# A decode-attention and gated-MLP kernel: two heads scored at a time, wider rows for v and wq, one softmax per pair of heads

## The chip, the cores and the metric

The kernel runs on one core of a Trainium2 chip. Its engines are TensorE (PE in the profile, with its weight loads as PEld), VectorE (DVE), ScalarE (ACT), GpSimd (POOL) and SyncE (SP), which issues all loads here. The metric is the device time in microseconds of one execution, the median of several runs.

## The reference

One token is decoded. A gate mixes an attention over a long cache with a gated MLP, all in float32:

```python
x: (1, 1, 512)   k_cache, v_cache: (1, 8, 32768, 128)   wq: (512, 4096)   wo: (4096, 512)
w1, w3: (512, 1792)   w2: (1792, 512)

g = sigmoid((x * gate_w).sum(-1))
q = (x @ wq) as 32 query heads of 128          # 4 query heads share one head of the cache
p = softmax(q . k * 128 ** -0.5)               # over 32768 keys
a = (p . v as one row of 4096) @ wo
b = (silu(x @ w1) * (x @ w3)) @ w2
out = g * a + (1 - g) * b                      # (1, 1, 512)
```

The two caches are 134.2 MB each, wq and wo 8.4 MB each, w1, w3 and w2 3.7 MB each: 296 MB to load for a result of 512 numbers.

## The kernel before, in words

**Units.** Each of the 8 cache heads (`HKV`) is cut into four units of 8,192 keys (4 MB). In a unit of k, each of the 128 partitions holds 64 keys of 128 numbers, one contiguous row of 32 KB. The k rows of one load lie 128 KB apart in memory (`kd`, partition p has 256 keys in a row and unit m takes 64 of them); the v rows of one load lie side by side (`vd`).

**Buffers and the load queue.** One pool `stream` has four buffers of 32 KB a partition, and `load` (lines 67 to 70) takes the next one for every k, v, wq half, w1, w3 and w2. All loads are issued by SyncE, in the order of the program. SyncE waits at each until the buffer that it takes has been read by its last reader: for k that is VectorE's transpose (line 187), for v TensorE's matmul (line 288). wo comes per head in rows of 8 KB, through a pool of two buffers (`load_wo`, line 270); for the last head in rows of 2 KB.

**The loop.** It runs 37 times: in step i it issues k unit i and v unit i - 5 (`LAG`), works off k unit i in four quarters, and then v unit i - 5. w1 and w3 come in steps 2 and 3.

**Scores** (`scores`, line 184). For a quarter c of the 128 numbers of each key, VectorE turns the unit in blocks of 32 x 32 (`kt`, line 187, two buffers), and four matmuls, one for each group of 32 columns of the array, multiply it with the head's query window `win` (line 194; x8 in the profile, since a float32 matmul is recorded as two). After the fourth quarter ScalarE copies the bank into `sb` (line 201).

**Softmax.** It is spread over later steps. `defer(n, fn)` puts a function n ticks on, and `tick` runs what is due; there is one tick after each quarter. When a head's four units are scored, `flip` (line 207) brings keys to the partitions, in two banks of eight matmuls each, one tick apart; `top` takes maxima (219); `maxima`, `diagonal` and `spread_max` bring the maximum over all partitions to all of them (229, 234, 236, 241), one tick each; `softmax` (245) has ScalarE write eight exponentials of 128 x 128 into `prob`, each with its sum by accumulator; `norm` and `invert` make the reciprocal of the sums. The order of the instructions of an engine is that of the program (a manual schedule), so what stands ahead in it and waits holds up all that is behind it on that engine.

**Values** (`values`, line 280). 16 matmuls per v unit add to one bank `o`; after the fourth unit ScalarE copies it to a row (294). `heads` (300) sums over groups, `scaled` (306) multiplies with the reciprocal, `quarter` (318) and `quartered` (325) spread the head over the partitions as wo's rows need it, `mix` (335) multiplies with wo in 16 matmuls of 128 columns, and `added` (342) adds to `acc`, each one tick after the other.

**Queries** (line 142). 32 matmuls with x as weights, on two halves of wq, give the queries in two banks. `spread` (157) copies each bank four times and turns it by 16 matmuls; `windows` (171) writes `win` in four copies for each bank.

**The end.** The last v unit comes in three pieces; w2 follows in four pieces of 5, 5, 3 and 1 rows a partition. VectorE multiplies w2's first five rows with the hidden numbers and adds them up in `sv` (443, 445), TensorE the other nine (458), and the last instruction joins the MLP with `acc` by the gate (467). The result is then stored.

Of the kernel before, what the change touches and what calls it, by code (L numbers as in the profile page):

```python
# [15 lines left out]
LAG = 5  # L16
# [3 lines left out]
def kernel(  # L20
# [24 lines left out]

    NB = 64
    UK = NB * P
    NU = S // UK
    UNITS = HKV * NU
    FR = F // P  # L50
    FJ = F // 4
    assert DH == P and D == 4 * P and REP == 4 and NU == 4 and HKV == 8 and F == FR * P
# [7 lines left out]
    ps_o = ctx.enter_context(tc.tile_pool(name="ps_o", bufs=2, space=bass.MemoryType.PSUM))  # L60
    ps_m = ctx.enter_context(tc.tile_pool(name="ps_m", bufs=4, space=bass.MemoryType.PSUM))
# [5 lines left out]
    def load(name, n, src):  # L67
        t = stream.tile([P, NB * DH], F32, tag="stream", name=name)
        nc.sync.dma_start(t[:, 0:n], src)
        return t  # L70
# [5 lines left out]
    QW = NC * HQ * DH // 2  # L76
    wq_t = [load("wq0", QW, wqd[:, 0:QW])]
    nc.sync.dma_start(xs, x.rearrange("a b (p c) -> p (a b c)", p=P))
    nc.sync.dma_start(gw, gate_w.rearrange("(p c) -> p c", p=P))
    wq_t.append(load("wq1", QW, wqd[:, QW:2 * QW]))  # L80
# [6 lines left out]
    sel = ident[:, 0:P:32]  # L87
# [4 lines left out]
    nc.vector.tensor_copy(  # L92
        pick.rearrange("p (g x) -> p g x", g=4), ident.rearrange("p (g x) -> p g x", g=4)[:, :, 0:16]
    )


    quad = const.tile([P, 4, 4, 32], F32, name="quad")
    for q in range(4):
        nc.vector.tensor_copy(quad[:, :, q, :], ident.rearrange("p (x k) -> p k x", k=4))
# [5 lines left out]
    win = const.tile([P, HKV, 4, 32], F32, name="win")  # L105
    nc.vector.memset(win, 0.0)
    prob = [const.tile([P, 65 * 16], F32, name=f"prob{b}") for b in range(2)]
    otp = [const.tile([P, REP, 32], F32, name=f"otp{b}") for b in range(2)]
    for b in range(2):
        nc.gpsimd.memset(prob[b][:, 1024:1040], 0.0)  # L110
        nc.gpsimd.memset(otp[b], 0.0)
    acc = const.tile([P, P], F32, name="acc")
    nc.gpsimd.memset(acc, 0.0)
    gate = const.tile([P, 2], F32, name="gate")
    htp = const.tile([P, FR, 32], F32, name="htp")
    nc.gpsimd.memset(htp, 0.0)
# [25 lines left out]
    def queries():  # L142
        pq = [misc(f"pq{b}") for b in range(2)]
        for c in range(NC):
            for b in range(2):
                for j in range(4):
                    o = ((c % 2) * HKV + 4 * b + j) * REP * DH
                    nc.tensor.matmul(  # L148
                        pq[b][32 * j:32 * j + 32, :], xp[:, c, :], wq_t[c // 2][:, o:o + REP * DH],
                        start=(c == 0), stop=(c == NC - 1),  # L150
                    )
        for b in range(2):
            qs = work.tile([P, 512], F32, tag="ob", name=f"qs{b}", bufs=2)
            nc.scalar.copy(qs, pq[b])  # L154
            defer(4 * b, spread, b, qs)

    def spread(b, qs):
        rp = ktp.tile([P, 16, P], F32, tag="kt", name=f"rp{b}")
        for r in range(4):
            nc.vector.tensor_copy(  # L160
                rp[:, :, 32 * r:32 * r + 32], qs.rearrange("p (a j) -> p a j", a=16)
            )
        pt = misc(f"pt{b}")
        for a in range(16):
            nc.tensor.matmul(pt[:, 4 * a:4 * a + 4], rp[:, a, :], sel, start=True, stop=True)  # L165
        if b == 0:
            windows(b, pt)
        else:
            defer(1, windows, b, pt)

    def windows(b, pt):
        for r in range(4):
            nc.vector.tensor_copy(
                win[32 * r:32 * r + 32, 4 * b:4 * b + 4, :, 4 * r:4 * r + 4],
# [32 lines left out]
    def flip(h, f, mx):  # L207
# [6 lines left out]
        if f == 0:  # L214
            defer(1, flip, h, 1, mx)
# [281 lines left out]
```

## Time and profile before

| what | value |
| --- | --- |
| median of 3 runs | 701.78 us (701.48 to 702.08) |
| the profiled execution's own time | 704.29 us |
| its span, first to last instruction | 702.4 us |
| granted TensorE clock, mean | 0.737 |
| loaded | 296.23 MB, 422 GB/s over the span |
| ScalarE, GpSimd busy | 69.2 us (10%), 1.6 us (0%) |

The span is what the profile sees; what lies around it (1.9 us) is start and end of the execution. A group of the profile has a line, an engine, an operation, the tiles written and read, the count, the busy time, the mean of one, and the idle time ahead with what ended it. In the timeline, the first two columns are the start and the length in microseconds. For a load, "us to landing" counts from its issue by SyncE to its arrival. A clock of 0.50 is TensorE at half speed.

### The profile page before, as it was taken

How to read it: one execution, taken by the hardware profiler on the slowest of the kernel's cores; microseconds unless marked ns; L12 is line 12 of the kernel's file. 1: busy time of each engine (PE TensorE's matmuls, PEld its weight loads, DVE VectorE, ACT ScalarE, POOL GpSimd, SP SyncE). 2: the span in 40 equal slices, each digit the busy share in tenths (PEclk: the TensorE clock that was granted, in tenths of full speed). 3: DMA queues.
4: the chain of work that ended last, by engine and by line, in shares of the span. 5: the costliest groups of instructions: out<-in, count | busy, mean ns of one | idle time of the engine just before them, and what ended most of it. 6: DMA issues, size and time to landing. Idle time of an engine off the chain costs nothing.

```text
span 702.4 us, 6858 instructions
## 1 busy us (share of the span) xinstructions
PE 464.2 (66%) x3038; PEld 176.7 (25%) x3038; DVE 326.4 (46%) x274; ACT 69.2 (10%) x175; POOL 1.6 (0%) x12
## 2 busy tenths in 40 slices
PE   2667778856874497545964589745955568748746
PEld 0331152204220042202320143202322142203314
DVE  1078548554653444553543455552643547532002
ACT  0100102100200002000020003000020002000100
POOL 0000000000000000000000000000000000000000
PEclk9766865895676759876687756877598757678885
DMA  9999999999999999999999999999999999999994
GB/s 377 424 435 427 439 425 431 430 428 437 425 436 425 437 426 434 427 428 433 428 425 438 432 431 432 423 439 426 431 430 432 429 435 427 429 436 425 426 418 177
DMA packets 12517, 296.67 MB, mean 422 GB/s; under 512 B 1604, under 2 KB 1608, under 8 KB 2376
## 3 DMA queue, kind: packets, MB, share of 16 engines
q1 hardware_dynamic: 12488, 296.23, 98.4%
q8 instruction: 24, 0.39, 0.2%
q14 instruction: 5, 0.04, 0.0%
HBM read 296.23 MB, written 0.00 MB: 422 GB/s over the span
## 4 chain that ended last, share of the span: by engine, by line
DMA 55%; PE 14%; DVE 12%; issue 1%; SPq 0%; ACT 0%; DVEq 0%
DMA k<-in_A_k_cache_dram 45%; DVE kt L187 11%; DMA v<-in_A_v_cache_dram 9%; PE pf L210 6%; PE s L194 5%; PE o L288 2%; PE pa L335 1%; DVE mx L219 1%; PE pb L458 0%; DVE sv L445 0%; PE po L300 0%; DVE m L224 0%; SPq L410 0%; ACT ob L294 0%; DVE acc L342 0%
## 5 line engine op out<-in xcount | busy, mean ns | idle before, releaser
L187 DVE STREAM_TRANSPOSE kt<-k 128x2048 f32<-128x2048 f32 x128 | 289.6, 2291 | 215.5 <-DMA k<-in_A_k_cache_dram 213.3
L194 PE MATMUL s<-kt,win 128*32 128x512 f32 x1024 | 196.8, 853 | 195.8 <-DVE kt L187 188.0
L288 PE MATMUL o<-v,prob 128*32 128x512 f32 x1024 | 140.0, 695 | 13.7 <-DMA v<-in_A_v_cache_dram 13.7
L194 PEld LDWEIGHTS s<-kt,win 128*32 128x32 f32 x1024 | 25.6, 127 | 303.0 <-issue 160.5
L201 ACT COPY sb<-s 128x512 f32<-128x512 f32 x32 | 35.4, 1105 | 485.3 <-PE s L194 485.3
L288 PEld LDWEIGHTS o<-v,prob 128*32 128x32 f32 x1024 | 35.3, 127 | 105.1 <-issue 82.0
L210 PEld LDWEIGHTS pf<-pick,sb 128*128 128x128 f32 x256 | 52.5, 313 | 24.1 <-issue 24.1
L210 PE MATMUL pf<-pick,sb 128*128 128x64 f32 x256 | 55.3, 406 | 0.0
L219 DVE TENSOR_REDUCE mx<-pf 128x4 f32<-128x512 f32 x16 | 11.1, 691 | 47.5 <-PE pf L210 47.5
L251 ACT ACTIVATE prob<-pf,nm 128x128 f32<-128x128 f32 x64 | 23.4, 498 | 26.7 <-DVE nm L247 26.7
L148 PE MATMUL pq<-wq,xp 128*32 128x512 f32 x64 | 12.1, 922 | 17.7 <-DVE xp L104 13.5
L251 ACT ACTIVATION_READ_ACCUMULATOR prob<-pf,nm 128x1 f32 x64 | 14.8, 232 | 0.0
L308 DVE TENSOR_TENSOR otp<-po,recip 128x4 f32<-128x4 f32 x1 | 0.2, 165 | 28.5 <-PE po L300 28.5
L335 PE MATMUL pa<-wo,otp 128*32 128x128 f32 x256 | 13.0, 365 | 0.3 <-DVE otp L308 0.3
L335 PEld LDWEIGHTS pa<-wo,otp 128*32 128x32 f32 x256 | 11.1, 151 | 7.2 <-issue 6.7
L165 PE MATMUL pt<-ident,rp 128*128 128x4 f32 x64 | 10.9, 307 | 1.8 <-DVE rp L160 1.8
L165 PEld LDWEIGHTS pt<-ident,rp 128*128 128x128 f32 x64 | 10.8, 267 | 3.5 <-issue 3.5
L294 ACT COPY ob<-o 128x512 f32<-128x512 f32 x8 | 4.7, 585 | 71.0 <-PE o L288 71.0
L300 PEld LDWEIGHTS po<-fold,ob 128*128 128x128 f32 x64 | 8.6, 208 | 9.1 <-ACT ob L294 9.1
L318 PEld LDWEIGHTS pk<-on,quad 128*128 128x128 f32 x56 | 8.9, 243 | 6.7 <-issue 6.7
L300 PE MATMUL po<-fold,ob 128*128 128x4 f32 x64 | 9.3, 268 | 1.4 <-ACT ob L294 1.4
L160 DVE COPY rp<-qs 128x512 f32<-128x512 f32 x8 | 2.8, 416 | 15.1 <-ACT qs L154 15.1
(61 smaller groups left out, 102.0 us busy)
## 6 DMA issues: line engine op xcount, KB each, us to landing
k<-in_A_k_cache_dram SPq DMA_DIRECT2D x32, 4096.0 KB, 29.7
v<-in_A_v_cache_dram SPq DMA_DIRECT2D x31, 4096.0 KB, 33.1
wq<-in_A_wq_dram SPq DMA_DIRECT2D x2, 4096.0 KB, 16.9
wo<-in_A_wo_dram SPq DMA_DIRECT2D x8, 1024.0 KB, 27.0
w<-in_B_w_dram SPq DMA_DIRECT2D x2, 3584.0 KB, 25.8
w<-in_B_w_dram SPq DMA_DIRECT2D x2, 1280.0 KB, 29.6
v<-in_A_v_cache_dram SPq DMA_DIRECT2D x1, 2048.0 KB, 31.3
v<-in_A_v_cache_dram SPq DMA_DIRECT2D x2, 1024.0 KB, 34.4
```

Source lines behind the costliest of these rows:

```text
L148: nc.tensor.matmul(pq[b][32 * j:32 * j + 32, :], xp[:, c, :], wq_t[c // 2][:, o:o + REP * DH], start=(c == 0), stop=(c == NC - 1),)
L165: nc.tensor.matmul(pt[:, 4 * a:4 * a + 4], rp[:, a, :], sel, start=True, stop=True)
L187: nc.vector.transpose(kt.rearrange("p (n i) -> p n i", i=32), kin.rearrange("p (n c j) -> p c n j", c=4, j=32)[:, c],)
L194: nc.tensor.matmul(s_ps[0][32 * g:32 * g + 32, :], win[:, h, c, :], kt[:, 512 * g:512 * g + 512], start=(c == 0), stop=(c == 3),)
L201: nc.scalar.copy(sb[h][:, :, :, m], s_ps[0].rearrange("p (n i) -> p n i", i=32))
L210: nc.tensor.matmul(pf[h, f][:, 64 * a:64 * a + 64], sb[h][:, 8 * f + a].rearrange("p i m -> p (i m)"), pick, start=True, stop=True,)
L219: nc.vector.tensor_reduce(mx[:, f, :], pf[h, f].rearrange("p (n q) -> p q n", q=REP), axis=AX.X, op=ALU.max)
L251: nc.scalar.activation(prob[h % 2][:, 0:1024].rearrange("p (a n q) -> p a n q", a=16, q=REP)[:, :, 8 * f:8 * f + 8, q], pf[h, f].rearrange ...
L288: nc.tensor.matmul(o_ps[0][32 * t:32 * t + 32, :], prob[h % 2][:, o:o + 32], vt[:, n * P:(n + 4) * P], start=(r == 0 and g == 0), stop=(r ...
L300: nc.tensor.matmul(po[:, 0:REP], ob[:, b * P:(b + 1) * P], fold[:, 4 * b:4 * b + 4], start=(b == 0), stop=(b == 3),)
L318: nc.tensor.matmul(pk[:, 4 * k:4 * k + 4], quad[:, k].rearrange("p q x -> p (q x)"), on, start=True, stop=True)
L335: nc.tensor.matmul(pa[32 * j:32 * j + 32, 0:P], otp[h % 2][:, q, :], wo_t[h][:, q, j * P:(j + 1) * P], start=(q == 0), stop=(q == REP - 1),)
```

## The change

It reorganizes the work by pairs of heads:

- **Scores of two heads.** A pair's 65,536 keys are cut into 8 parts, each in 128 rows of 32 KB that now lie 256 KB apart: the lower half of the partitions holds one head, the upper half the other. `win` is per pair, and one pass of matmuls scores both. A step s handles two parts (`half`), so there are 16 steps.
- **Buffers.** The pool of four 32 KB buffers is split: `narrow` (two of 32 KB) takes the two k parts of a step, `wide` (one of 64 KB) takes wq as one load of 8 MB, then w1 with w3, then the k parts of step 2, then v: half a head (8 MB) at a time, in rows of 64 KB. `v13` and `v15` go through `narrow` instead, the latter's end in the old pieces. w2 goes through `wide`.
- **Order.** Step s issues v of step s and k of step s + 4, does `values` of step s and then the scores of step s + 4. Four k steps stand ahead of all that.
- **One softmax per pair,** at once after the pair's last scores: flips in four banks, maxima, subtraction by VectorE from the banks into rows, exponentials of 128 x 256 by ScalarE. The sums are taken by VectorE from `prob` (`total`), without accumulator reads. `values` of the next step follows behind it. `prob`, `sb` and the sums exist once per head of a pair or once in all.
- **wo** comes per pair in rows of 16 KB through one buffer (the last pair in 2 KB rows); `place`, `placed`, `mix` do a pair at once: 8 matmuls of 128 x 8, two vector steps, 8 matmuls of 512 columns. For the last pair, each head is mixed by itself.
- **Queries** are turned by a VectorE transpose, without `spread`'s copies and matmuls; 16 small copies write `win`.
- **MLP and end.** The hidden row is turned by VectorE; the gate is multiplied into `recip` and the hidden numbers, so `acc` (now 128 x 512) adds everything up; w2 comes in pieces of 4, 4, 4 and 2 rows.
- PSUM: `ps_o` has one bank in place of two, four banks hold the flips, `misc` has one in place of four.

```diff
-    stream = ctx.enter_context(tc.tile_pool(name="stream", bufs=4))
-    proj = ctx.enter_context(tc.tile_pool(name="proj", bufs=2))
+    narrow = ctx.enter_context(tc.tile_pool(name="narrow", bufs=2))
+    wide = ctx.enter_context(tc.tile_pool(name="wide", bufs=1))
+    proj = ctx.enter_context(tc.tile_pool(name="proj", bufs=1))
...
+    wq_t = in_wide("wq", (0, 2 * R, wqd))
...
+    def windows(b, qs):
+        qt = ktp.tile([P, NB * 32], F32, tag="kt", name=f"qt{b}")[:, 0:512]
+        nc.vector.transpose(qt, qs)
...
+    def scores(w, m, z, kin):
+        for c in range(4):
+            kt = ktp.tile([P, NB * 32], F32, tag="kt", name=f"kt{w}_{m}_{z}_{c}")
+            nc.vector.transpose(
...
+            for g in range(4):
+                nc.tensor.matmul(
+                    s_ps[0][32 * g:32 * g + 32, :], win[:, w, c, :], kt[:, 512 * g:512 * g + 512],
...
+            if c == 3:
+                nc.scalar.copy(sb[:, :, z, :, m], s_ps[0].rearrange("p (n i) -> p n i", i=32))
+            tick()
...
+    def softmax(w):
+        mx = work.tile([P, 4, 8], F32, name="mx")
+        for f in range(4):
+            pf[f] = bank(f"pf{w}_{f}")
+            for a in range(8):
+                nc.tensor.matmul(
+                    pf[f][:, 64 * a:64 * a + 64],
+                    sb[:, 8 * (f % 2) + a, f // 2].rearrange("p i m -> p (i m)"), pick,
+                    start=True, stop=True,
+                )
+            nc.vector.tensor_reduce(
+                mx[:, f, :], pf[f].rearrange("p (n q) -> p q n", q=8), axis=AX.X, op=ALU.max
+            )
+        m1 = work.tile([P, 8], F32, name="m1")
+        nc.vector.tensor_reduce(m1, mx.rearrange("p f q -> p q f"), axis=AX.X, op=ALU.max)
+        pr = misc(f"pr{w}")
+        nc.tensor.transpose(pr[0:8, 0:P], m1, ident)
+        mr = work.tile([8, 1], F32, name="mr")
+        nc.vector.tensor_reduce(mr, pr[0:8, 0:P], axis=AX.X, op=ALU.max)
+        md = work.tile([8, 8], F32, name="md")
+        nc.vector.tensor_scalar(md, ident[0:8, 0:8], mr, None, op0=ALU.mult)
+        pb = misc(f"pb{w}")
+        nc.tensor.matmul(pb[:, 0:8], ones[0:8, :], md, start=True, stop=True)
+        top = work.tile([P, 8], F32, name="top")
+        nc.vector.tensor_copy(top, pb[:, 0:8])
+        for f in range(4):
+            d = row(f"d{w}_{f}")
+            nc.vector.tensor_tensor(
+                d.rearrange("p (n q) -> p n q", q=8), pf[f].rearrange("p (n q) -> p n q", q=8),
+                top.unsqueeze(1).to_broadcast([P, 64, 8]), op=ALU.subtract,
+            )
+            for u in range(2):
+                nc.scalar.activation(
...
+                    AF.Exp, scale=SCALE,
+                )
+        for u in range(2):
+            defer(1, total, w, u)
+        defer(2, norm, w)
...
+    def values(h, e, z, vt, groups=range(4)):
...
+    kd = k_cache.rearrange("a (w u) s d -> w (a u s d)", u=2).rearrange("w (p m z r) -> w m z p r", p=P, m=4, z=2)
+    vd = v_cache.rearrange("a h (e p n) d -> (a h) e p (n d)", e=2, p=P)
...
+    kt0 = keys_narrow(0)
+    ff["w"] = None
+    queries()
+    tick()
+    gate_part()
+    w13 = [t.rearrange("(p c) f -> p (c f)", c=NC) for t in (w1, w3)]
+    ff["w"] = in_wide("w13", (0, NC * F, w13[0]), (NC * F, 2 * NC * F, w13[1]))
+    half(0, kt0)
+    kt1 = keys_narrow(1)
+    ff_hidden()
+    k0, k1 = keys(2)
+    half(1, kt1)
+    t = in_wide("k2", (0, R, k0), (R, 2 * R, k1))
+    kt3 = keys_narrow(3)
+    half(2, (t[:, 0:R], t[:, R:2 * R]))
+    half(3, kt3)
+    softmax(0)
+
+    for s in range(2 * HKV):
+        h, e = divmod(s, 2)
+        src = vd[h, e]
+        if s < 2 * HKV - 3 or s == 2 * HKV - 2:
+            t = in_wide(f"v{s}", (0, 2 * R, src))
+            parts = (t[:, 0:R], t[:, R:2 * R])
...
+        if s + 4 < 2 * HKV:
+            kt0 = keys_narrow(s + 4)
+        if s % 4 == 1:
+            load_wo(s // 4)
+        for z in range(2):
+            values(h, e, z, parts[z])
+        if s + 4 < 2 * HKV:
+            half(s + 4, kt0)
+            if s % 4 == 3:
+                softmax(s // 4 + 1)
+        elif s < 2 * HKV - 1:
+            for _ in range(6):
+                tick()
```

`in_narrow` and `in_wide` take the next buffer of their pool and issue one load for each piece; `row` is a 128 x 512 tile of two buffers; `heads` is as before, and runs in the tick after a head's last values; `scaled`, `place`, `placed`, `mix` and `added` follow one tick each, for both heads of a pair from `place` on.

More of the change, by code (lines that the diff above doesn't have):

```diff
@@ L460, in ff_down @@
             )
[L462 to L465 removed]
+    for k in range(8, FR):
+        if k == 12:
+            ff_down(ones[:, 0:32], acc)
+        ff_down(htp[:, k, :], w2t[:, k, :], first=(k == 8), last=(k == FR - 1))
     res = const.tile([P, P], F32, name="res")
[L467 removed]
+    nc.vector.tensor_copy(res, pb[:, 0:P])
     nc.sync.dma_start(out.rearrange("a b (j e) -> (a b j) e", e=P), res[0:P:32, :])
```

414 lines of the change are left out of this document (159 added, 255 removed).

## The prediction

> **What bounds the kernel now.** I read the page's DMA part first, then the slices, then what the DMA issues waited for.
>
> ```profile
> PE 464.2 (66%) x3038; PEld 176.7 (25%) x3038; DVE 326.4 (46%) x274; ACT 69.2 (10%) x175; POOL 1.6 (0%) x12
> GB/s 377 424 435 427 439 425 431 430 428 437 425 436 425 437 426 434 427 428 433 428 425 438 432 431 432 423 439 426 431 430 432 429 435 427 429 436 425 426 418 177
> DMA packets 12517, 296.67 MB, mean 422 GB/s; under 512 B 1604, under 2 KB 1608, under 8 KB 2376
> q1 hardware_dynamic: 12488, 296.23, 98.4%
> DMA 55%; PE 14%; DVE 12%; issue 1%; SPq 0%; ACT 0%; DVEq 0%
> k<-in_A_k_cache_dram SPq DMA_DIRECT2D x32, 4096.0 KB, 29.7
> v<-in_A_v_cache_dram SPq DMA_DIRECT2D x31, 4096.0 KB, 33.1
> ```
> ```profile
> SPq L69 <- DVE kt L187: 337.4, 32, 22.6
> SPq L69 <- PE o L288: 151.0, 27, 9.4
> ```
> ```profile
> 455.00:495.00 40.00, 21.78 (x131) 7.98 (x124) 16.36 (x8) 1.14 (x1) 0.00 (x0) 0.71 1.00 431
> ```
>
> (The last three columns of the window's row are granted clock, DMA share, GB/s.) The one load queue is busy for 98.4% of 16 engines' span, 691 of 702.4 us, and in the middle stretch its share is 1.00. A load lands about 30 us after its issue, three times the 9.73 us that 4.194 MB take at 431 GB/s: there are always two or three more behind it. SyncE waits long for a buffer (337 and 151 us), yet the engines never run dry. So **the bytes are the bound**, at 296.23 MB / 691 us = 428.6 GB/s. TensorE (66%) and VectorE (46%) only have to give buffers back in time. The change can win what it takes off the load engines, and lose whatever time it lets them stand.
>
> **The rows.** v and wq now come in rows of 64 KB: 14 of the 16 v loads (`v13` and `v15` stay narrow) and wq, 15 x 128 = 1,920 rows where 3,840 of 32 KB were. The cost of a row follows from the lines above. At 431 GB/s a 32 KB row occupies an engine for 32,768 B x 16 / 431 GB/s = 1.216 us. All bytes as 32 KB rows would be 9,040 rows, or 10,996 us; the queue's busy time is 16 x 691.2 = 11,059 us. The remaining 62 us belong to the other 12,488 - 9,040 packets: 18 ns each (an estimate; the rounding of 431 moves it by 5). 1,920 packets fewer on 16 engines save 1,920 x 18 ns / 16 = **2 us**. Below is nothing, if a 64 KB row goes out as two packets; above, 125.8 MB at 439 GB/s (the best slice of the row above) in place of 428.6 would be 7 us. I take 2, being a price per packet. The wo rows get longer but the last ones (2 KB) double in number: nothing.
>
> **The buffers.** Four 32 KB buffers were shared by everything. Now two narrow ones hold k, and one wide one holds v, so the loads run v (19.46 us), k, k (9.73 each), and the next v can't start until `values` has read the last. In a usual round that takes 64 matmuls after landing, with 19.46 us of k queued behind: 9 us of cover. VectorE turns both k in about 18 us of a 38.9 us round. These rounds cost nothing.
>
> **The softmax.** It was spread over deferred steps, with values running five loads late. Now it stands as one block after the last k of a pair, ahead of the next `values` in TensorE's order, and that `values` needs its result. So four times the wide buffer is held from the landing of the last k until transposes, last scores, flips, maxima, exponentials and 64 value matmuls are through. Meanwhile one v and two k can load: 38.9 us. Behind the waiting v load on SyncE stand the next two k loads, though their buffers are free by then; behind the block's steps on VectorE the next transposes, and on TensorE `values` and the next scores, which catch up in the 20 us that a round leaves them. What else goes or comes (the accumulator reads on ScalarE, the quarter copies, `total`, the subtraction, `recip` times gate) lies beside loads under way and costs nothing while the load queue is full; in the block it is counted. The rows for each link, at full and at half clock:
>
> ```profile
> 626.20 8.96 DVE L187 STREAM_TRANSPOSE kt<-k 128x2048 f32<-128x2048 f32 x4 [11.07 <-DMA k<-in_A_k_cache_dram]
> 628.66 1.93 PE L194 MATMUL s<-kt,win 128*32 128x512 f32 x8 [8.98 <-DVE kt L187]
> 633.02 1.07 PE L194 MATMUL s<-kt,win 128*32 128x512 f32 x8 [0.32 <-DVE kt L187]
> 165.72 3.68 PE L210 MATMUL pf<-pick,sb 128*128 128x64 f32 x16
> 639.64 3.79 PE L210 MATMUL pf<-pick,sb 128*128 128x64 f32 x32
> 616.06 3.62 PE L288 MATMUL o<-v,prob 128*32 128x512 f32 x32
> 645.56 5.34 PE L288 MATMUL o<-v,prob 128*32 128x512 f32 x32 [0.88 <-DMA v<-in_A_v_cache_dram]
> 191.01 1.87 PE L318 MATMUL pk<-on,quad 128*128 128x4 f32 x8
> 644.40 0.27 PE L229 MATMUL pr<-ident,m 128*4 128x128 f32 x1 [0.98 <-DVE m L224]
> 644.71 0.28 DVE L234 TENSOR_REDUCE mr<-pr 4x1 f32<-4x128 f32 x1 [0.36 <-PE pr L229]
> 645.03 0.22 DVE L236 TENSOR_SCALAR md<-ident,mr 4x4 f32<-4x4 f32 x1
> 652.58 0.38 PE L241 MATMUL pb<-md,ones 4*128 4x4 f32 x2
> 653.07 0.16 DVE L247 TENSOR_SCALAR nm<-pb 128x4 f32<-128x4 f32 x1 [0.22 <-PE pb L241]
> 653.27 0.48 ACT L251 ACTIVATE prob<-pf,nm 128x128 f32<-128x128 f32 x1 [1.73 <-DVE nm L247]
> 0.74 0.39 SPq L69 DMA_DIRECT2D wq<-in_A_wq_dram  x1
> ```
> ```profile
> L210 PE MATMUL pf<-pick,sb 128*128 128x64 f32 x256 | 55.3, 406 | 0.0
> L219 DVE TENSOR_REDUCE mx<-pf 128x4 f32<-128x512 f32 x16 | 11.1, 691 | 47.5 <-PE pf L210 47.5
> ```
> ```profile
> 163.50:177.00 13.50, 12.88 (x56) 7.61 (x56) 7.37 (x7) 0.00 (x0) 0.00 (x0) 0.50 1.00 432
> 639.60:643.40 3.80, 3.80 (x36) 3.65 (x32) 0.69 (x1) 0.00 (x0) 0.00 (x0) 1.00 1.01 427
> 0.00:10.00 10.00, 0.00 (x0) 0.00 (x0) 1.86 (x8) 1.28 (x1) 1.64 (x12) 1.00 0.90 360
> ```
>
> Four transposes take 9.0 us, the last scores 1.07 or 1.93. The flips are 4 x 16 matmuls (x16 in 3.68 us at clock 0.50, x32 in 3.79 at 1.00): 7.6 or 14.7 us. Then one by one: the reduction 0.69, a small one about 0.25, transpose 0.27, maximum 0.28, diagonal 0.22, spread 0.38, copy about 0.2, subtraction about 0.7 (a bank, as in the 691 ns row), three exponentials of 256 elements about 0.5 each (0.48 for 128 strided ones), ten handovers of some 0.06: 5.1 us (an estimate from these rows). The 64 value matmuls take 2 x 3.62 = 7.2, or 10.7 with the clock half for most of them (2 x 5.34).
>
> For pairs 1 to 3 the steps of the head before (`place`, 16 matmuls; `mix`, 16 of 512 columns) lie between these scores, and VectorE's `placed` and `added` wait for them with the transposes queued behind. At half clock a quarter's scores and `place` take 1.93 + 2 x 1.87 = 5.7 us against 2.25 for a transpose, and so do scores and `mix` (16 columns of 512 by the x32 row, doubled): waits of about 3.45 us twice. At full clock they are about 0.65 each. With the two steps' own 1.1 us, less 0.7 of slack per load, this adds 1.7 or 7.3 us.
>
> The sums: pairs 1 to 3 need 9.0 + 1.7 + 1.1 + 7.6 + 5.1 + 7.2 = 31.7 us at full clock, and 9.0 + 7.3 + 1.9 + 14.7 + 5.1 + 10.7 = 48.7 at half; pair 0, without deferred steps, 30.0 and 41.4. From the 38.9 us go the issue (0.39) and the start and landing of a transfer, together some 1.4 us: in the first 10 us, with the issue at 0.74, the engines were busy for 0.90. That leaves 37.5. The idle time of the engines is 0 to 3.9 us for pair 0, 0 to 11.2 for pairs 1 and 2. Behind pair 3 a wo load (2.1 MB, 4.9 us) stands in the queue too, so 0 to 6.3 there.
>
> Which clock? Around the old flips it was 0.50 for 13.5 us while TensorE was busy for 12.88 of them: flips do not raise it. But a flip met at full clock kept it (639.6 to 643.4). Now 18 us of scores without a break come first, so full clock is likelier at the flips than before, though `place` and the pauses let it drop, and the 5 us chain lets it drop again before `values`. I take the middle of both sums and a little over, 41.5 us, for pairs 1 and 2: 4 us idle each; none for pairs 0 and 3 (middles 35.7 and 40.2, under 37.5 and 42.4). Together **8 us**, between 0 and 33.
>
> **Start and end.**
>
> ```profile
> 23.74 6.03 PE L148 MATMUL pq<-wq,xp 128*32 128x512 f32 x32 [4.21 <-DMA wq<-in_A_wq_dram]
> 687.28 1.89 PE L288 MATMUL o<-v,prob 128*32 128x512 f32 x8 [1.41 <-DMA v<-in_A_v_cache_dram]
> 689.85 1.87 PE L300 MATMUL po<-fold,ob 128*128 128x4 f32 x8 [0.69 <-ACT ob L294]
> 691.98 1.94 PE L335 MATMUL pa<-wo,otp 128*32 128x128 f32 x32 [0.26 <-DVE otp L308]
> 694.50 2.32 DVE L445 SCALAR_TENSOR_TENSOR sv<-w,htp,sv 128x512 f32<-128x512 f32 x3
> 699.31 0.35 DVE L467 SCALAR_TENSOR_TENSOR res<-pb,gate,acc 128x128 f32<-128x128 f32 x1 [2.48 <-PE pb L458]
> ```
>
> wq as one load lets the queries begin where their second half began (23.74) and run 2 x 6.03 us: the wide buffer is free for w1 and w3 at about 36 us. Two k loads cover this until 1 + 4 x 9.73 = 40 us; without that cover it would be up to the 12 us of queries. Turning the queries on VectorE takes the `spread` matmuls off that path. w1 and w3 are read before the two k loads behind them have landed, so they hold nothing up either. At the end, the last v piece is followed by values, row copy, heads, then 8 + 8 wide matmuls (about 3.8 us) beside four vector steps (3.0), one addition (0.7), 24 small matmuls (1.4) and a copy (0.3): 6.2 us after the heads, where 691.98 to 699.66 was 7.7. The last rows of w2 land about there in both. I take 0; it may be 1 either way.
>
> **The sum.** 702.4 - 2 + 8 = 708.4 us of span. The profiled execution's own time was 704.29 us, 1.9 over its span and 2.5 over the median of 701.78. The median follows the difference: 701.78 + 6 = **707.8 us**.
>
> **The rivals.**
> *No idle at all.* If the clock is at full speed when the flips begin, every chain is 31.7 us and ends 6 us inside its cover. For it: the 3.79 us row, and 18 us of scores ahead. Against: the old flips took 55.3 us for 16 blocks, 3.46 each, near the 3.68 of the half clock. The sum is then 702.4 - 2, a median of 699.8: not slower. It decides at a chain of 37.5 us. Chance 0.12.
> *The flips wake the clock themselves.* If a busy TensorE has to wait 3.4 us only (15 flips at 0.23 us, then 49 at 0.119), flips take 9.2 us and the chain is at most 36: again no idle, 699.8 us. Against it stands the 0.50 over 12.88 busy us. The Trainium skill has this as its rule ("TensorE: Matmul & The Clock Gate", Part 1: the gate opens after about 3.4 us of sustained matmuls); by it the 8 us of the sum would be 0, and the trace disagrees for flips, though scores did raise the clock. Chance 0.12.
> *Idle of 1 to 3 us in all.* Between both: about 702. Chance 0.10.
> *Half clock throughout.* 15 to 33 us of idle, 715 to 733 us. For it: 0.50 around the old flips. Chance 0.12.
> *k slows.* The rows of a k load now lie 256 KB apart, not 128. If that costs 3% of k's 134.2 MB / 428.6 GB/s = 313 us, it is 9 us more, and VectorE waits longer for k: about 711 without the idle. Nothing in the trace shows it, 431 GB/s holds at 128 KB. The Trainium skill ("DMA: Bandwidth & Descriptors", Latency and other measured facts) reports copies slowing at large power-of-two row pitches, from 512 KiB up; this kernel stays under, and no run here shows it yet. Chance 0.04.
> That a 64 KB row is split again is possible in every case (0.3), and adds 2 us.
>
> **How the numbers follow.** The forecast, idle of 3 to 14 us and 703 to 714 us, has 0.50. A measurement of this kernel can tell about 0.2%, 1.4 us. Faster by more than that: most of the two no-idle rivals, 0.19. Within: their rest, the 1 to 3 us case, a little of the forecast, 0.17. Slower: 0.64. The range of 8 in 10 runs from 699.3 to 717; the forecast's own is 703 to 714.
>
> **What would show it.** The DMA row should have dips at four places, after each softmax block (near 155, 310 and 470 us), of 0 to 10 us each; the chain of waits should run through flips and `values` there, and SyncE's wait for `values` should end late. Granted clock over the flips tells which sum holds. In a usual round the DMA share must stay 1.00. Packets near 10,300 tell that rows are whole, 12,200 that they are split. A drop of the rate below 428 GB/s in stretches full of k would show the pitch. Dips elsewhere (first 50 us, the end) would make the prediction wrong in its free parts.

## The result and the profile after

The changed kernel takes **710.79 us** (median of 6 runs, 707.90 to 723.33) where the kernel before, beside it, took 702.02 (6 runs, 701.48 to 703.12): a ratio of 1.0125 [1.0078, 1.0173], so it is slower by 0.8 to 1.7%. The profiled execution has 708.59 us, a span of 706.8 and a mean granted clock of 0.751. The ratios leave out executions more than 1.5% above the fastest of their kernel (here 723.33) and the medians hold them all, so below a median can stand further from 702 than its ratio says.

The lines of the page that answer to those of before are these:

```profile
GB/s 415 390 431 439 428 436 430 437 437 425 422 456 413 441 426 439 424 376 356 439 449 415 431 430 428 439 429 344 440 446 416 424 460 414 428 433 400 415 401 284
DMA packets 10290, 296.62 MB, mean 420 GB/s; under 512 B 1300, under 2 KB 1304, under 8 KB 2456
q1 hardware_dynamic: 10264, 296.23, 97.8%
DMA 59%; PE 19%; DVE 15%; issue 7%; ACT 0%; SPq 0%; DVEq 0%
```

The packets fell from 12,488 to 10,264 on the load queue, so the 64 KB rows go out whole. Its share fell from 98.4% of 702.4 us to 97.8% of 706.8: 691.2 us of work either way. The loads take as long as before, they only stand still in between: the slices at 300 to 336 us (376, 356) and at 477 to 495 us (344) have the dips that were forecast behind the blocks of pairs 1 and 2. The chain of waits now gives TensorE 19% (before 14%) and 7% to issue.

SyncE's waits for `values` have become fewer and longer (us in total, times, longest; before 151.0, 27, 9.4):

```profile
SPq L83 <- PE o L287: 137.6, 12, 21.3
```

And windows around the two dips (busy time by engine; the last three columns are granted clock, DMA share and GB/s):

```profile
284.00:309.80 25.80, 19.02 (x123) 9.49 (x115) 14.36 (x16) 2.54 (x4) 0.00 (x0) 0.76 0.97 415
309.80:320.00 10.20, 10.12 (x69) 4.85 (x73) 9.86 (x7) 2.29 (x8) 0.00 (x0) 0.73 0.59 252
478.00:488.00 10.00, 8.43 (x72) 3.48 (x64) 8.94 (x5) 0.00 (x0) 0.00 (x0) 0.94 0.75 293
```

Up to 309.8 us the load queue is as good as full (0.97 of all engines); in the ten microseconds of `values` behind that it is at 0.59. The timeline of this round shows why. It is the round in which `half` scores the last keys of pair 1; the first of its two k parts has just landed (the 20.16 is VectorE's idle time before it):

```profile
269.02 0.33 SPq L83 DMA_DIRECT2D v<-in_A_v_cache_dram  x1
269.39 4.50 DVE L193 STREAM_TRANSPOSE kt<-k 128x2048 f32<-128x2048 f32 x2 [20.16 <-DMA k<-in_A_k_cache_dram]
280.22 17.08 SPq L77 DMA_DIRECT2D k<-in_A_k_cache_dram  x2
283.54 0.23 DVE L326 TENSOR_TENSOR own<-pk,mask 128x64 f32<-128x64 f32 x1 [3.35 <-PE pk L319]
284.01 4.49 DVE L193 STREAM_TRANSPOSE kt<-k 128x2048 f32<-128x2048 f32 x2
291.85 0.69 DVE L344 TENSOR_TENSOR acc<-acc,pa 128x512 f32<-128x512 f32 x1 [3.34 <-PE pa L337]
292.45 4.50 DVE L193 STREAM_TRANSPOSE kt<-k 128x2048 f32<-128x2048 f32 x2
297.00 1.69 PE L200 MATMUL s<-kt,win 128*32 128x512 f32 x8 [0.29 <-DVE kt L193]
298.62 7.36 PE L216 MATMUL pf<-pick,sb 128*128 128x64 f32 x64
309.88 10.08 PE L287 MATMUL o<-v,prob 128*32 128x512 f32 x64 [1.50 <-ACT prob L243]
320.02 0.33 SPq L83 DMA_DIRECT2D v<-in_A_v_cache_dram  x1
```

The first part landed at 269.39, and the second follows in the queue 9.73 us later, at 279.1. From then on the queue holds only v (issued at 269.02) and the two k loads of the row x2 (the first at 280.22, the second 17 us later), 38.9 us of work: it is empty at 318.0. The next v load can be issued only at 320.02, when the 64 value matmuls have read the wide buffer. Between, VectorE waits 3.35 us for `place` and 3.34 us for `mix`, then come transposes, last scores, flips, the block, and `values`. By its packets all 16 load engines stood from 318.5 to 321.0 us, and again for 1.32 us at 483.5. Counted engine by engine and averaged, the standstill is 4.8 us behind block 1 (the softmax block of pair 1), 2.8 behind block 2, 1.2 behind block 3 and none behind block 0: 8.8 us.

### The profile page after: what moved, and what is told of

The parts are those of the page before. It is cut to its first block, busy times and chain, and to the rows that moved or that the text cites. A ratio compares the mean times of both kernels' runs of the same rounds, so it can differ in the third digit from the quotient of the medians.

```text
span 706.8 us, 6069 instructions
## 1 busy us (share of the span) xinstructions
PE 434.3 (61%) x2694; PEld 137.6 (19%) x2694; DVE 344.9 (49%) x256; ACT 55.5 (8%) x79; POOL 1.5 (0%) x10
## 3 DMA queue, kind: packets, MB, share of 16 engines
q1 hardware_dynamic: 10264, 296.23, 97.8%
## 4 chain that ended last, share of the span: by engine, by line
DMA 59%; PE 19%; DVE 15%; issue 7%; ACT 0%; SPq 0%; DVEq 0%
DMA k<-in_A_k_cache_dram 50%; DVE kt L193 12%; PE o L287 5%; PE pf L216 4%; PE s L200 4%; DMA v<-in_A_v_cache_dram 3%; DMA xs<-in_A_x_dram 3%; DMA w<-in_B_w_dram 3%; PE po L301 2%; PE pq L161 1%; PE pa L337 1%; PE pk L319 1%; DVE d L238 0%; DVE mx L221 0%; DVE sums L253 0%
## 5 line engine op out<-in xcount | busy, mean ns | idle before, releaser
L287 PE MATMUL o<-v,prob 128*32 128x512 f32 x1024 | 147.4, 729 | 106.7 <-DMA v<-in_A_v_cache_dram 100.7
L287 PEld LDWEIGHTS o<-v,prob 128*32 128x32 f32 x1024 | 44.3, 131 | 208.3 <-issue 139.4
L216 PEld LDWEIGHTS pf<-pick,sb 128*128 128x128 f32 x256 | 35.4, 227 | 5.1 <-issue 5.1
L216 PE MATMUL pf<-pick,sb 128*128 128x64 f32 x256 | 36.0, 312 | 0.0
L221 DVE TENSOR_REDUCE mx<-pf 128x8 f32<-128x512 f32 x16 | 11.1, 691 | 33.9 <-PE pf L216 33.9
L253 DVE TENSOR_REDUCE sums<-prob 128x4 f32<-128x1024 f32 x8 | 15.9, 2022 | 0.5 <-ACT prob L243 0.5
L243 ACT ACTIVATE prob<-d 128x256 f32<-128x256 f32 x32 | 10.7, 404 | 44.6 <-DVE d L238 44.0
L238 DVE TENSOR_TENSOR d<-pf,top 128x512 f32<-128x512 f32 x16 | 10.4, 688 | 1.1 <-ACT prob L243 0.8
L337 PE MATMUL pa<-wo,otp 128*32 128x512 f32 x56 | 10.2, 851 | 0.3 <-DVE otp L310 0.3
L319 PE MATMUL pk<-on,spot 128*128 128x8 f32 x48 | 7.5, 292 | 0.0
```

The source lines that it names most:

```text
L216: nc.tensor.matmul(pf[f][:, 64 * a:64 * a + 64], sb[:, 8 * (f % 2) + a, f // 2].rearrange("p i m -> p (i m)"), pick, start=True, stop=True,)
L221: nc.vector.tensor_reduce(mx[:, f, :], pf[f].rearrange("p (n q) -> p q n", q=8), axis=AX.X, op=ALU.max)
L243: nc.scalar.activation(prob[u][:, 0:1024].rearrange("p (z y n q) -> p z n y q", z=2, y=8, q=4)[:, f // 2, 8 * (f % 2):8 * (f % 2) + 8], d. ...
L253: nc.vector.tensor_reduce(sums[:, 4 * u:4 * u + 4], prob[u][:, 0:1024].rearrange("p (n q) -> p q n", q=4), axis=AX.X, op=ALU.add)
L287: nc.tensor.matmul(o_ps[0][32 * t:32 * t + 32, :], prob[u][:, o:o + 32], vt[:, n * P:(n + 4) * P], start=((e, z, g) == (0, 0, 0)), stop=(( ...
L319: nc.tensor.matmul(pk[:, 8 * k:8 * k + 8], spot[:, k].rearrange("p t x -> p (t x)"), on, start=True, stop=True)
```

## What the runs tell apart

The theory is that of the forecast: the single wide buffer is held through the softmax, and the load queue runs dry. The rivals are that the loads themselves are slower or dearer (64 KB rows, a pitch of 256 KB), and that a part costed at nothing (queries, start, end) costs the time. The kernel before took 702.0 to 702.5 us beside these (medians of 19 to 29 runs).

**x1_no_wait.** The first value step of each pair reads a constant, and the block stands behind it:

```diff
-    softmax(0)
...
-   o_ps[0][32 * t:32 * t + 32, :], prob[u][:, o:o + 32], vt[:, n * P:(n + 4) * P],
+   o_ps[0][32 * t:32 * t + 32, :], (flat if u == 0 and e == 0 else prob[u])[:, o:o + 32], vt[:, n * P:(n + 4) * P],
...
             values(h, e, z, parts[z])
+        if s % 4 == 0:
+            softmax(s // 4)
         if s + 4 < 2 * HKV:
             half(s + 4, kt0)
-            if s % 4 == 3:
-                softmax(s // 4 + 1)
```

> The first of a pair's four value steps multiplies v by a constant in place of the probabilities, so the output leaves a quarter of the attention's sum out; the softmax block then stands behind those value matmuls. All loads and all work stay, and the wide buffer no longer waits for a softmax. If the held wide buffer is the loss (theory 1): no dip of the DMA share after any block, 699 to 703 us, and runs within 1 us of each other. If the 64 KB rows or the 256 KB step of the k rows cost the time (theory 2): 707 to 711 us as in the changed kernel. If it is the start or the end of the kernel (theory 3): the same 707 to 711.

Measured: 701.95 us (699.47 to 703.58, 10 runs), ratio 0.9994 [0.9980, 1.0008]. The time is as the theory has it; the executions lie 4.1 us apart, though, where 1 us was expected. Its page, its timeline (the v load that stood at 320.02) and one window:

```profile
q1 hardware_dynamic: 10264, 296.23, 98.6%
```

```profile
305.90 0.33 SPq L83 DMA_DIRECT2D v<-in_A_v_cache_dram  x1
```

```profile
264.00:330.00 66.00, 47.47 (x307) 19.36 (x299) 36.67 (x30) 5.44 (x11) 0.00 (x0) 0.71 1.01 436
```

Nothing else of the change is taken back: rows, pitch, queries, start and end are those of the changed kernel, and so is all the work of the block. Only `values` does not wait for it. The v load goes out 14 us earlier, the queue is full through the stretch, and the slowdown is gone as a whole. (Near 495 us its load engines stand for 1.4 us each, where VectorE, now with the block behind `values`, is late with the k transposes.) That is the theory, and both rivals are out as a net cost.

**x2_two_halves.** The v load behind each block as two loads into the same tile:

```diff
-            t = in_wide(f"v{s}", (0, 2 * R, src))
+            cut = [(0, 2 * R)] if s % 4 != 1 else [(0, R), (R, 2 * R)]
+            t = in_wide(f"v{s}", *[(a, b, src[:, a:b]) for a, b in cut])
```

> Only the v load that stands behind each softmax block (v1, v5, v9; v13 was narrow already) is cut in two loads of 32 KB rows into the two halves of the wide buffer, so that its first half needs only the first half of the value matmuls. Theory 1: about 4 to 5 us more cover at each block, idle only where the clock is half nearly throughout: 700 to 704 us. Theory 2: three of fourteen loads have other rows, so 706 to 711. Theory 3: 707 to 711.

Measured: 709.44 us (705.63 to 717.26, 4 runs), ratio 1.0069 [1.0048, 1.0090]. A miss, and its timeline says why:

```profile
310.17 10.14 PE L287 MATMUL o<-v,prob 128*32 128x512 f32 x64 [1.50 <-ACT prob L243]
320.36 0.80 SPq L83 DMA_DIRECT2D v<-in_A_v_cache_dram  x2
```

Both loads (x2) go out together behind the last value matmul. A tile of the pool is released as a whole, so cutting the load alone frees nothing earlier; the buffer has to be two tiles.

**x7_two_tiles.** The wide buffer as two tiles of 32 KB, for wq, w1 and w3 and the k of step 2 too:

```diff
-    wide = ctx.enter_context(tc.tile_pool(name="wide", bufs=1))
+    wide = ctx.enter_context(tc.tile_pool(name="wide", bufs=2))
...
-            t = in_wide(f"v{s}", (0, 2 * R, src))
-            parts = (t[:, 0:R], t[:, R:2 * R])
+            parts = [in_wide(f"v{s}_{z}", (0, R, src[:, z * R:z * R + R])) for z in range(2)]
```

> The wide buffer is two tiles of 32 KB a partition, each with its own load of 32 KB rows and its own release, all else as in the changed kernel. In the run with two loads into one tile both were issued only after the last value matmul; here the first can start when the first half of the values is through, 3.5 to 5 us earlier, and covers the second. Theory 1: 701 to 705 us. If whole rows of 64 KB save 2 us, that is lost here, 703 to 707; by the loads alone it is under 0.5 us. Theory 2 (now out): under 702 at once.

Measured: 704.99 us (700.41 to 719.11, 12 runs), ratio 1.0013 [0.9997, 1.0030]. The profiled execution has a span of 707.3 us and one dip, where the flips of block 2 met the half clock:

```profile
461.03 13.92 PE L216 MATMUL pf<-pick,sb 128*128 128x64 f32 x64
479.15 10.17 PE L287 MATMUL o<-v,prob 128*32 128x512 f32 x64 [1.50 <-ACT prob L243]
485.94 3.76 SPq L83 DMA_DIRECT2D v<-in_A_v_cache_dram  x2
```

The first half of v is now issued after half of `values` (485.94, with values from 479.15), about 3.4 us earlier than the end of values. That closes the gap behind block 1 (flips of 7.36 us, no standstill), and not the one behind block 2 (flips of 13.92 us: all load engines stood for 7.3 us at 479.6). So part of the wait goes, and the spread of the executions stays.

**x3_place_later.** The steps `place` to `added` eight ticks later, out of the way of the last scores:

```diff
-            defer(1, place, h)
+            defer(8, place, h)
```

> The deferred steps place, placed, mix and added of the pair before come eight ticks later, in the step after the softmax block, so that they no longer lie between the scores ahead of it. Theory 1: the block ends 2 to 7 us earlier for pairs 1 to 3, idle mostly gone: 700 to 704 us. Theories 2 and 3: 707 to 711.

Measured: 704.16 us (701.17 to 711.69, 10 runs), ratio 1.0036 [1.0008, 1.0065], just over the 700 to 704 expected. In the profiled execution (702.55 us, one of its shorter ones) no dip is left behind blocks 1 and 2; a small one came near 640 us (window 628 to 650: DMA share 0.91). **x8_tiles_later** joins this line with the two tiles of x7 and has no other edit:

> The two tiles of 32 KB, and place, placed, mix and added eight ticks later. Theory 1: each block ends at least 5 us inside its cover even with the clock half for part of it: no dips, 699.5 to 702 us, all runs within 3 us. If something else than the held buffer is left: 704 us or more.

Measured: 704.35 us (701.64 to 712.57, 12 runs), ratio 1.0043 [1.0017, 1.0070]. Again a miss, with the same new dip (window 636 to 646: DMA share 0.54):

```profile
638.05 3.24 PE L337 MATMUL pa<-wo,otp 128*32 128x512 f32 x16 [0.30 <-DVE recip L264]
641.36 0.39 SPq L277 DMA_DIRECT2D wo<-in_A_wo_dram  x1
641.80 1.12 SPq L83 DMA_DIRECT2D v<-in_A_v_cache_dram  x2
```

That is a wait of my edit's own making. For pair 2 the later `mix` runs only at 638.05. It holds the one wo buffer, so the last pair's wo load is issued at 641.36, and the next v load (641.80) stands behind it on SyncE, although its buffer was free. In x3 the same wo load went out at 638.64.

**x11_two_pairs_later** therefore moves the steps of pairs 0 and 1 only, with the two tiles, and **x12_wide_later** does so with the single 64 KB tile:

```diff
-            defer(1, place, h)
+            defer(8 if h < 5 else 1, place, h)
```

> Two tiles of 32 KB; place and what follows come later for the first two pairs only. In the run where all three came later, the last pair's wo load waited for the late mix of the pair before and held the v loads behind it on SyncE (issued at 641.4 us, with 1.1 us of idle engines). Theory 1 with this second wait: no dips, 699.5 to 702.5 us, runs within 3 us. If the late steps cost something else: 704 us as there.

> The changed kernel with its 64 KB tile and 64 KB rows; place and what follows come later for the first two pairs only. Theory 1: blocks 1 and 2 end 2 to 7 us earlier, but the buffer is still released as a whole: 701 to 704 us, idle only where the flips run at half clock (13.9 us). Against the run with two tiles it should be 0 to 3 us slower; if 64 KB rows have a gain of their own, up to 2 us faster in runs without idle.

x11: **701.03 us** (700.25 to 703.35, 12 runs), ratio 0.9990 [0.9980, 0.9999]. x12: 705.80 us (699.31 to 711.06, 12 runs), ratio 1.0013 [0.9984, 1.0041], above the 701 to 704 expected. The load row of x11 (the queue is busy for 99.0%, the most of all kernels here that compute) and one of its blocks:

```profile
q1 hardware_dynamic: 12424, 296.23, 99.0%
```

```profile
290.76 13.92 PE L216 MATMUL pf<-pick,sb 128*128 128x64 f32 x64
309.17 9.54 PE L287 MATMUL o<-v,prob 128*32 128x512 f32 x64 [1.88 <-ACT prob L243]
315.33 3.76 SPq L83 DMA_DIRECT2D v<-in_A_v_cache_dram  x2
```

In x11 even a block with flips at half clock (13.92 us) leaves the queue without a common standstill: scores and flips begin 8 us earlier than in the changed kernel (290.76 against 298.62), and the first v tile is refilled at 315.33. In x12 the same block at half clock costs (window 310 to 322: DMA share 0.75; x11: 0.96). Its profiled execution (710.15 us, one of its longest) loses more behind block 3, whose steps are not moved: there the flips met half clock too, and all load engines stood for 4.1 us (window 645 to 655: DMA share 0.49). The fastest executions of x12, 699.3, are as fast as any. The two edits are each worth something alone, and only both together take the long executions away. x11 is the best version found: 1.4% under the changed kernel, and at most 0.2% under the one before.

**x4_loads.** Loads alone, in five stretches of 67.1 MB: v in 64 KB rows, v in 32 KB rows side by side, v in 32 KB rows 64 KB apart, k with rows 128 KB apart, k with rows 256 KB apart. All else is taken out; in its place stands, through two tiles of 64 KB:

```diff
+    for s in range(8):
+        put(v64[s // 2, s % 2])
+    for s in range(8):
+        put(v32[2 * s], v32[2 * s + 1])
+    for s in range(8):
+        put(*[v64[4 + s // 2, s % 2][:, z * R:z * R + R] for z in range(2)])
+    for s in range(8):
+        put(k128[s // 2, 2 * (s % 2)], k128[s // 2, 2 * (s % 2) + 1])
+    for s in range(8):
+        put(k256[s // 4, s % 4, 0], k256[s // 4, s % 4, 1])
```

> Loads alone, nothing is computed (the output is zeros): five stretches of 67.1 MB each through two buffers of 64 KB a partition: v in 64 KB rows; v in 32 KB rows side by side; v in 32 KB rows 64 KB apart; k in 32 KB rows 128 KB apart; k in 32 KB rows 256 KB apart. Theories 1 and 3: all five take 155 to 157 us, the first about 0.4% less than the second. Theory 2: the first or the last takes at least 1% more than the second and fourth, 157.5 us or more.

Measured (one run, 782.53 us), a window inside each stretch:

```profile
4.00:156.00 152.00, 0.00 (x0) 0.00 (x0) 1.00 1.00 435
159.00:311.00 152.00, 0.00 (x0) 0.00 (x0) 1.00 1.00 431
314.00:466.00 152.00, 0.00 (x0) 0.00 (x0) 1.00 1.00 431
469.00:622.00 153.00, 0.00 (x0) 0.00 (x0) 1.00 1.00 432
625.00:776.00 151.00, 0.00 (x0) 0.00 (x0) 1.00 1.00 431
```

By their packets, from one multiple of 67.1 MB landed to the next, the stretches take 155.8, 155.4, 155.4, 155.6 and 155.4 us; the first holds the start of the queue with its slow first packets. Within the stretches a 64 KB row takes an engine 2,420 ns and a 32 KB row 1,217 (means), 14 ns less than twice: behind those first packets, and with the packets at a window's edges counted by their part, 433.8 GB/s against 431.9. For the 125.8 MB of v and wq that would be 1.3 us. The pitch costs nothing: 431.7 GB/s at 128 KB, 431.8 at 256 KB.

**x5_flips_twice.** A dose: the flips of each block are done twice, which adds 7.15 us at full clock and 13.65 at half to each chain.

```diff
-            for a in range(8):
+            for a in 2 * list(range(8)):
```

> Every flip of the softmax block is done twice (the same numbers into the same bank): 64 more matmuls for each block, 7.4 us at full clock, 14.7 at half; the loads are the same. Theory 1 (the block holds the wide buffer past its cover): blocks 1 and 2, which already end late, give all of it on, 7.4 us or more each, blocks 0 and 3, which end some 3 us inside their cover, a part: 725 to 742 us. If the block is off the path and the idle time has another cause: at most 2 us more, 708 to 713.

Measured: 750.64 us (740.32 to 759.52, 4 runs), ratio 1.0576 [1.0543, 1.0609]. The median is above the 725 to 742 us expected: in the profiled execution (756.10 us, one of the longer ones) blocks 2 and 3 met half clock, where the dose is 13.65 us. The load rates and the flips of blocks 0 and 3:

```profile
GB/s 389 421 440 428 432 434 447 413 381 436 451 415 423 438 442 419 371 223 411 424 443 440 421 437 430 424 23 387 417 442 419 441 421 460 403 393 5 396 425 265
```

```profile
129.05 14.51 PE L216 MATMUL pf<-pick,sb 128*128 128x64 f32 x128
```

```profile
655.93 27.57 PE L216 MATMUL pf<-pick,sb 128*128 128x64 f32 x128
```

The slices at 23 and 5 GB/s are the standstills behind blocks 2 and 3. All load engines stood for 0.11, 10.75, 18.83 and 19.23 us behind the four blocks; counted engine by engine it is 1.6, 12.1, 20.1 and 20.5. Behind block 1, where the flips took 14.51 us in place of 7.36, this count grew from 4.8 to 12.1 us: 7.3 us for 7.15. Once the cover is used up, a microsecond in the block costs a microsecond. Behind block 0, without steps of a pair before it, the same dose costs 1.6: this chain had some 5.5 us of slack, where the forecast had 7.5 at full clock (30.0 against 37.5).

**x6_kept_busy.** 24 recorded matmuls of no use stand between the small steps of the block, to keep the clock up for `values`:

```diff
+        busy(4)
         m1 = work.tile([P, 8], F32, name="m1")
...
+        busy(2)
         mr = work.tile([8, 1], F32, name="mr")
...
+        busy(6)
         top = work.tile([P, 8], F32, name="top")
```

> 24 matmuls of 512 columns that nobody reads are put where TensorE waits in the softmax block (8 after the flips, 4 after the transpose, 12 after the spread), so that its clock is still full when values begin: the 64 value matmuls then take about 7.1 us, not 9.6 to 10.1. Theory 1 with the clock as the price: each block ends up to 3 us earlier, 703 to 708 us, and the runs where the clock is half before the flips stay. If the clock drop does not matter: 708 to 712.

Measured: 711.84 us (705.43 to 718.36, 4 runs), ratio 1.0058 [1.0038, 1.0079]. Inconclusive in its time. In its profile the v load behind block 1 goes out at 318.12, 1.9 us earlier than in the changed kernel, and all load engines stand for 0.38 us there in place of 2.45. But in block 2 the flips met half clock (13.92 us), and all load engines stood for 3.70 us at 481.6. The clock of `values` is worth about 2 us a block; what the flips meet is worth more, and this edit does not set it.

**x13_early_flips.** x11, with half of the flips moved between the last scores, so that the chain behind them is shorter:

```diff
+            if m == 3 and z == 1 and c in (1, 2):
+                flips(w, c - 1)
+            if m == 3 and z == 1 and c in (2, 3):
+                peak(c - 2)
```

> As with two tiles and two pairs later, and the first two of the four flips of a block, which need only the first of the last two k loads, are done between the quarters of the second. The block behind the last scores is then two flips, 3.7 us (full clock) or 7.0 us (half), shorter. Theory 1: no idle in any run, 699.5 to 702 us, like the kernel without the wait; the quarters may be held up by 1 to 4 us there, inside the cover.

Measured: 702.75 us (701.67 to 706.65, 12 runs), ratio 1.0012 [1.0002, 1.0022]. No gain, rather a loss of 1.7 us against x11, and above the 699.5 to 702 expected. Its block 2:

```profile
449.91 3.68 PE L217 MATMUL pf<-pick,sb 128*128 128x64 f32 x16
455.38 3.68 PE L217 MATMUL pf<-pick,sb 128*128 128x64 f32 x16
462.10 7.09 PE L217 MATMUL pf<-pick,sb 128*128 128x64 f32 x32 [1.18 <-ACT sb L205]
473.30 10.14 PE L296 MATMUL o<-v,prob 128*32 128x512 f32 x64 [1.50 <-ACT prob L252]
```

The early flips run at half clock (16 in 3.68 us), the scores beside them too (1.94 us for eight), and so do the 32 that are left (7.09 us, where 64 took 7.36 at full clock). Block 0 ran the same way. In block 1 the 32 flips that were left had full clock (3.79 us), and in block 3 the clock fell while they ran (5.37 us). That the moved flips took away the unbroken scores that had raised the clock is argued from blocks 0 and 2, not shown.

## Why the prediction was right, and where its sizes were off

The mechanism, the place, the sign and the case came as forecast; 710.79 us is in the forecast's own range of 703 to 714. How near the sum comes to the profile is in part luck, as the terms below show.

**The bound and the usual rounds: right.** 691.2 us of load work in both kernels; outside the rounds behind a block the queue stays full, and x1 takes the whole slowdown away with the wait.

**The chain: right nearly to the microsecond, partly by terms that cancel.** From the landing of the last k (279.1) to the issue of v (320.02) are 40.9 us, against 41.5 in the forecast, and the 38.9 us of cover from there end at 318.0, as counted. The terms: VectorE begins on the last k at 284.01, 4.9 us late, and spends 12.9 us on its four transposes with `mix` and `added` between; 9.0 of these 17.8 us are the transposes and 8.8 what the steps of the pair before cost, where the sums had 1.7 (full clock) and 7.3 (half). The two waits of 3.35 and 3.34 us are the forecast's 3.45 of the half clock. Last scores 1.7, flips 7.36 (7.6 in the sum). From the flips' end (305.98) to the first value matmul (309.88) 3.9 us, not 5.1: reductions run beside the flips, and of the exponentials only the first is in the way. Values 10.1 (10.7 at half clock).

**The clock: right for the flips of blocks 0 to 2.** It was full there, and half for the first part of `values` (5.6 of 10.1 us in block 1). Under `place` and `mix` it differed: half for both in block 1 (3.58 us each), half for `mix` alone in block 2, and full for both in block 3, whose flips then met half clock:

```profile
445.42 1.95 PE L319 MATMUL pk<-on,spot 128*128 128x8 f32 x16
451.93 3.60 PE L337 MATMUL pa<-wo,otp 128*32 128x512 f32 x16
462.42 7.36 PE L216 MATMUL pf<-pick,sb 128*128 128x64 f32 x64
623.81 13.92 PE L216 MATMUL pf<-pick,sb 128*128 128x64 f32 x64
```

So the middle of both sums fits block 1; no block was at one clock throughout. Block 3's longer cover, with the wo load and the narrow `v13`, left 1.2 us.

**The idle time: right in sum.** Forecast 4 and 4 us behind blocks 1 and 2 and none behind 0 and 3; measured 4.8, 2.8, 1.2 and 0: 8.8 against 8. Since the clock that a block meets differs from execution to execution, so close a sum is luck for this one.

**The rows: nearly right, and given back.** The term was 2 us, at 18 ns a packet; x4 shows 14 ns, 1.3 us by its rates. In the kernel next to nothing is left of it, 691.3 us of load work before and 691.0 after by the packets: the first packets after a standstill are slow, 0.5 to 0.7 us per engine at each of the three. x1, with 1.4 us of standstill in all but its start and end, has 98.6% of 700.2, 690.4 us. The forecast had no term for this. Where nothing stands still the gain may be there: the four shortest executions of x12 (64 KB rows) took 699.31 to 699.83 us, those of x11 (32 KB rows) 700.25 to 700.37. They differ in the release of the tiles too, so this is not shown.

**The end: mis-sized.** The term was 0, "1 either way". From the start of the last value matmuls to the end of the span it was 15.1 us before (687.28 to 702.4) and is 12.3 now:

```profile
694.47 1.07 PE L287 MATMUL o<-v,prob 128*32 128x512 f32 x8 [1.42 <-DMA v<-in_A_v_cache_dram]
703.84 0.29 DVE L475 COPY res<-pb 128x128 f32<-128x128 f32 x1 [1.77 <-PE pb L466]
```

That is 2.8 us less. By the packets, the last bytes land in both about 8.1 us behind the start of those matmuls (695.4 and 702.6); what follows them took 7.0 us and takes 4.2. But the clock over the end, in a window of before and one of after,

```profile
690.00:702.40 12.40, 8.15 (x120) 6.73 (x120) 4.40 (x9) 0.00 (x0) 0.00 (x0) 0.50 0.20 83
```
```profile
690.00:706.80 16.80, 10.14 (x112) 3.29 (x104) 4.07 (x7) 0.59 (x1) 0.00 (x0) 0.90 0.67 278
```

was 0.50 and 0.90. The later runs have the same end and tell chain and clock apart: from the last landing on, x11 took 4.1 us at full clock, as this execution did, and x8 and x13 took 5.4 us at half, the clock of the 7.0 before. So some 1.5 us of the 2.8 belong to the shorter chain and 1.3 to the clock that this execution met. With them the sum for the profiled executions is 702.4 + 8.8 - 2.8 = 708.4, against 706.8 measured. Of the 1.6 us that are left, 1.5 are the engines' common end (below): in the 25 us ahead of the last landing a load engine stood for 2.8 us on average before and for 1.3 after. The forecast span, 708.4 too, thus comes within 1.6 us of the 706.8 partly by luck: it counted 2 us for rows that did not come, and left out 4.3 us at the end.

**The step that failed is the last one, "The median follows the difference".** The profiled executions differ by 4.3 us (708.59 - 704.29), the medians by 8.8. The profiled execution of before was a long one (704.29 where the others lie between 701.48 and 703.12), that of after one of the short ones of its kernel. The executions of the changed kernel differ by 15 us (707.90 to 723.33; the mean clock is 0.756 in the shortest and 0.730 in the longest, but 0.744 at 708.98 as at 716.50), those before by 1.6. A block whose flips meet half clock costs up to 6.6 us, and which blocks do differs from execution to execution: blocks 0 to 2 were at full clock here, while in x7's profile blocks 2 and 3 were at half. x11, which no longer cares, has 3.1 us of spread. That this explains the executions of 716.5 and 723.3 is argued, not shown: they have no trace.

**The rivals.** *No idle at all* is out for this kernel, and is what x11 reaches and x1 nearly. *Idle of 1 to 3 us in all* is out in the profile: 8.8. *The flips wake the clock themselves* is out: 128 flips without a break ran at half clock for 27.57 us (x5). The Trainium skill's rule of about 3.4 us of sustained matmuls ("TensorE: Matmul & The Clock Gate", Part 1) does not hold for these. (The forecast's chain of "at most 36" for this rival was too low as well: with the steps of the pair before at half clock the forecast's own rows give 9.0 + 7.3 + 1.9 + 9.2 + 5.1 + 7.2 = 39.7.) *Half clock throughout* did not come in the profile; the execution of 723.3 may be it. *k slows* is out: 431.7 GB/s at a pitch of 128 KB, 431.8 at 256 KB (x4). The Trainium skill's slowing at large pitches ("DMA: Bandwidth & Descriptors", Latency and other measured facts) begins at 512 KiB, and no run here goes there.

## What to carry to other kernels

Where the load queue is the bound, write down for each buffer how long it is held from landing to its last reader, and what is queued behind it in that time: here 41 us against 39, in two places of a 700 us kernel, decided the result. Merging small steps into one block on the path of a held buffer pays nothing when they were hidden before, and it makes the time depend on the clock that the block happens to meet. Two tiles of half the size, and moving unrelated steps out of the block (but not past a load that waits for them), gave all of it back.

## What the runs showed that was not expected

- Flips (64 columns behind 128 new weights) did not raise the clock, and in the changed kernel and x5 they kept the one that they met: 64 in 7.36 or 13.92 us, 128 in 14.51 or 27.57. They do not hold a full clock in every case: in block 3 of x13 32 flips, behind a pause of 1.2 us, began at one every 0.11 us and ended at one every 0.21. A TensorE that the profile shows as busy throughout is not enough for the full clock.
- The 16 load engines drift apart in one unbroken queue. By the packets of before, they run out of work up to 5.8 us apart at its end; after, the first packets behind a standstill end together (within 0.6 us at 324), and the engines run out within 2 us. The standstills are not the only cause: x11, which has none, ends within 3.9 us, and x3, with one small dip, within 2.5. What else narrows the end stays open.
- After a standstill the first packets are slow, 0.5 to 0.7 us per engine at 320, 480 and 650 us.
